# Soft-cap attention and soft mixture of experts on one core: a new plan for exponentials, joined tanhs, loads and unused products

## The chip, the cores and the metric

The kernel runs on one core of one Trainium2 chip. The metric is the device time of one execution in microseconds (us), the median of several runs. Of the core's engines the text speaks of TensorE (PE, matrix products into PSUM; PEld is its loading of weights), VectorE (DVE), ScalarE (ACT), GpSimd (POOL) and SyncE (SP, which here only issues DMAs). Each engine works off its own queue in program order and waits there for semaphores of the others.

## The reference

Two stages in float32. Attention with capped scores, for 8 batches, 12 heads, 448 tokens and 64 values a head:

```python
scores = scale * np.matmul(q, k.transpose(0, 1, 3, 2))
scores = cap * np.tanh(scores / cap)
scores = scores - np.max(scores, axis=-1, keepdims=True)
attn = np.exp(scores)
attn = attn / (np.sum(attn, axis=-1, keepdims=True) + 1e-09)
return np.matmul(attn, v).astype(np.float32)
```

Its output, as a matrix x of 3584 tokens by 768, goes through a soft mixture of 8 experts with 4 slots each: logits `x @ phi`, their softmax over the tokens mixes x into 32 slot inputs, each expert applies two weight matrices with a ReLU between (768 to 1024 to 768), and the softmax of the logits over the slots mixes the slot outputs back into the tokens.

## The kernel before

Heads are taken in pairs, 48 of them; two pairs make a group of four heads (Q, 24 of them) that is loaded together. A pair has seven tiles of scores of 128 keys by 448 queries, 336 tiles in all, and six tiles make a chunk (j, 56 of them), worked on in two halves of three tiles. Three groups are a batch, and a batch takes seven chunks, so the plan repeats with j modulo 7.

In a chunk, TensorE makes the scores in PSUM (`qk_chunk`, L337 on, six matmuls for a half), ACT takes the tanh out of PSUM into SBUF (`tanh_chunk`, L354, the activation at L365 for one half), and then the exponential in place (`exp_part`, L373). Chunks named in JOINED (L380) have one tanh over all six tiles (L361); for these both halves of scores must be there. From chunk 10 to chunk 49 the scores have one buffer of six banks, of which each half is free again when its tanh is over.

VectorE takes over part of the exponentials: SHARED (L381) says of each chunk how many of its six tiles, and `poly_exp` (L603) does them by a polynomial in seven instructions, steps 0 to 6 at L609 to L616. POLY (L382 to L590) says in which chunk and slot each step is issued. ACT does the tiles that are left.

Two chunks later TensorE multiplies with v (`pv_first`, `pv_rest`, L654 and L671; matmuls at L634), VectorE divides by the sums (`norm`, a reciprocal at L641 and a product at L644), and side jobs follow: `x_transp` turns the result (L689), `logits`, `e_exp` (an exponential of the logits on ACT, L721), `slot_sums`, `e_transp` (its copy ET at L740) and `e_sums` for a batch. `transp` (L269) turns the next k and q (matmuls kps and qps at L278, copies kT and qT by VectorE at L280). `vcast` (L285) casts v on GpSimd and lets SP load the next v; `load` (L182) issues the loads of k and q on GpSimd's queue, where the loads of the experts' weights (L116, L120) stand too.

The order is written out by hand. The main loop (L899 to L932) runs through a chunk as slots: `0`, tanh of the first half, `m`, tanh of the second half, `e`, the exponential of the chunk before, the first value products, `a`, their tail, the next chunk's first half of scores, `b`, the rest of the value products with slot `r` between the reciprocal and the product, `c`, the second half of scores, `d`. After a joined tanh the first half of scores comes only behind the rest of the value products. `at` puts a job into a slot of a chunk; `<` and `>` are ahead of and behind the slot's other jobs. WHEN (L818) has the slots of side jobs by chunk of the batch: `k1` to `q3` the turning of k and q of the batch's groups, `lk1` to `lq3` the loads of the group after, `x`, `lg`, `ee`, `ss`, `et`, `es` the side jobs.

TensorE also does products that nobody uses: `busy` (L878), `spare` (L800, in an own PSUM tile, 384 or 128 columns each) and `fill` (L660, 57 columns each, in the columns that the value products leave free). FILL (L804) places those that repeat with each batch.

The first pair is prepared apart (`first_pieces`, L224, called at L249): its float32 k and q are cast, turned and copied in pieces on ACT, VectorE and TensorE. SP loads q, and ACT's queue loads the first pair's k in two parts (L209). GpSimd's queue has its memsets first, then the q and k loads of group 2 (L260 to L262).

After chunk 55 comes the tail (L933 on): the last value products, the experts' two layers (L1078, L1106) and the mixing back with the stores of the output (L1130 to L1206).

Of the kernel before, what the change touches and what calls it, by code (L numbers as in the profile page):

```python
# [20 lines left out]
NT = 7  # L21
# [3 lines left out]
CS = 3  # L25
# [12 lines left out]
def kernel(  # L38
# [185 lines left out]
    def first_pieces(h, jobs):  # L224

        for stage, nm, c0, c1, eng, bank, at0 in jobs:
            copy = act.copy if eng is act else dve.tensor_copy
            cols = slice(h * HP, h * HP + HP)
            if stage == "junk":
                busy(c0)  # L230
            elif stage == "cast":
                copy(casts[nm, 0][:, c0:c1, cols],
                     raws[nm, 0][h][:, c0 * DH:c1 * DH].rearrange("p (c d) -> p c d", d=DH))
            elif stage == "turn":
                for c in range(c0, c1):
                    pe.transpose(bank[cols, at0 + c - c0, :], casts[nm, 0][:, c, cols], ident)
            else:
                copy(qkT[nm, 0][cols, c0:c1, :], bank[cols, at0:at0 + c1 - c0, :])  # L238

    def first_half(h):  # L240
# [5 lines left out]
        if h == 0:  # L246
# [128 lines left out]
    def exp_chunk(j):  # L375
# [4 lines left out]
    JOINED = (10, 14, 17, 21, 24, 31, 35, 38, 42, 45, 49)  # L380
    SHARED = {1: (2, 0), 3: (3, 0), 4: (3, 0), 6: (2, 0), 7: (3, 0), 9: (3, 0), 11: (3, 0), 12: (3, 0), 14: (3, 0), 16: (3, 0), 18: (3, 0), 19: (3, 0), 21: (3, 0), 23: (3, 0), 25: (3, 0), 26: (3, 0), 28: (3, 0), 30: (3, 0), 32: (3, 0), 33: (3, 0), 35: (3, 0), 37: (3, 0), 39: (3, 0), 40: (3, 0), 42: (3, 0), 44: (3, 0), 46: (3, 0), 47: (2, 0), 48: (2, 0), 49: (3, 0), 51: (2, 0), 52: (1, 0), 53: (3, 0), 54: (1, 0)}  # L381
    POLY = {(1, 'm'): ((1, 0),),  # L382
            (1, '<b'): ((1, 1),),
            (1, '>d'): ((1, 2),),
            (2, '<a'): ((1, 3),),
            (2, '>b'): ((1, 4),),
            (2, '<d'): ((1, 5),),
            (3, 'm'): ((3, 0),),
            (3, 'e'): ((3, 1),),
            (3, '>a'): ((1, 6),),  # L390
            (3, '<b'): ((3, 2),),
            (3, '<d'): ((3, 3),),
            (4, 'm'): ((3, 4),),
            (4, '<b'): ((3, 5),),
            (4, '>c'): ((4, 0),),
            (5, 'm'): ((4, 1),),
            (5, 'e'): ((3, 6),),
            (5, '<a'): ((4, 2),),
# [3 lines left out]
            (6, 'e'): ((4, 5), (6, 1)),  # L402
            (6, '<a'): ((4, 6),),
            (6, '>b'): ((6, 2),),
            (7, 'm'): ((6, 3),),
            (7, 'e'): ((6, 4), (7, 0)),
            (7, '<a'): ((6, 5),),
            (7, '<d'): ((7, 1),),
            (8, '0'): ((7, 2),),
            (8, 'm'): ((7, 3),),  # L410
            (8, '<a'): ((6, 6),),
            (8, '>b'): ((7, 4),),
            (8, '>c'): ((7, 5),),
            (9, 'e'): ((9, 0),),
            (9, '<a'): ((7, 6),),
            (9, '>b'): ((9, 1),),
            (9, '>d'): ((9, 2),),
            (10, 'm'): ((9, 3),),
            (10, '>b'): ((9, 4),),
            (10, '<d'): ((9, 5),),  # L420
            (11, 'm'): ((11, 0),),
            (11, 'e'): ((9, 6),),
            (11, '>a'): ((11, 1),),
# [3 lines left out]
            (12, '>a'): ((12, 0),),  # L427
            (12, '<b'): ((11, 5),),
            (12, '<c'): ((12, 1),),
            (13, '<a'): ((12, 2),),  # L430
            (13, '>a'): ((11, 6),),
            (13, 'r'): ((12, 3),),
            (13, '<d'): ((12, 4),),
            (14, '0'): ((12, 5),),
            (14, '<a'): ((14, 0), (12, 6)),
            (14, '>a'): ((14, 1),),
            (14, '<d'): ((14, 2), (14, 3)),
            (15, '<b'): ((14, 4),),
            (15, '>d'): ((14, 5),),
            (16, '0'): ((14, 6),),  # L440
            (16, '<b'): ((16, 0),),
            (16, '>c'): ((16, 1),),
            (16, '>d'): ((16, 2),),
            (17, 'e'): ((16, 3),),
            (17, '<a'): ((16, 4),),
            (17, '>d'): ((16, 5),),
            (18, 'm'): ((18, 0),),
            (18, '<a'): ((16, 6),),
            (18, '>a'): ((18, 1),),
            (18, '>b'): ((18, 2),),  # L450
            (18, '>d'): ((18, 3),),
            (19, '0'): ((18, 4),),
            (19, 'e'): ((18, 5), (19, 0)),
            (19, '<c'): ((18, 6),),
            (19, '>c'): ((19, 1),),
            (19, '<d'): ((19, 2),),
            (19, '>d'): ((19, 3),),
# [6 lines left out]
            (22, '<d'): ((21, 5),),  # L464
            (23, 'm'): ((23, 0), (21, 6)),
            (23, 'e'): ((23, 1),),
            (23, '<d'): ((23, 2),),
            (24, '0'): ((23, 3),),
            (24, 'm'): ((23, 4),),
            (24, '>c'): ((23, 5),),  # L470
            (25, 'm'): ((25, 0),),
            (25, '<a'): ((25, 1), (23, 6)),
            (25, '>b'): ((25, 2),),
            (25, '<c'): ((25, 3),),
            (25, '>d'): ((25, 4), (25, 5)),
            (26, '>b'): ((25, 6),),
            (26, '<c'): ((26, 0),),
            (27, 'm'): ((26, 1),),
            (27, 'e'): ((26, 2),),
            (27, '>b'): ((26, 3), (26, 4)),  # L480
            (28, 'e'): ((26, 5), (28, 0)),
            (28, '<a'): ((26, 6),),
            (28, '<c'): ((28, 1),),
            (28, '>c'): ((28, 2),),
            (29, '>a'): ((28, 3),),
            (29, '<b'): ((28, 4),),
            (29, '<d'): ((28, 5),),
            (30, 'e'): ((28, 6),),
            (30, '>b'): ((30, 0),),
            (30, '>c'): ((30, 1),),  # L490
            (31, '0'): ((30, 2),),
            (31, 'm'): ((30, 3),),
            (31, '<b'): ((30, 4),),
            (31, '>d'): ((30, 5),),
# [4 lines left out]
            (33, '0'): ((32, 3),),  # L499
            (33, 'e'): ((32, 4),),  # L500
            (33, '<b'): ((32, 5),),
            (33, '>b'): ((33, 0),),
            (33, '<c'): ((33, 1),),
            (34, '0'): ((33, 2), (33, 3)),
            (34, '>b'): ((33, 4),),
            (34, '<c'): ((32, 6), (33, 5)),
            (35, '<a'): ((33, 6),),
            (35, '<b'): ((35, 0),),
            (35, '>b'): ((35, 1),),
            (35, '<c'): ((35, 2),),  # L510
            (36, '<a'): ((35, 3),),
            (36, '>a'): ((35, 4),),
            (37, 'm'): ((35, 5), (35, 6)),
            (37, '<a'): ((37, 0),),
            (37, '>a'): ((37, 1),),
            (38, 'e'): ((37, 2),),
            (38, '>a'): ((37, 3),),
            (38, '>b'): ((37, 4),),
            (38, '>c'): ((37, 5),),
            (39, 'e'): ((39, 0), (37, 6)),  # L520
            (39, '>a'): ((39, 1),),
            (39, '>b'): ((39, 2),),
            (39, '<c'): ((39, 3),),
            (39, '>c'): ((39, 4),),
            (40, '>a'): ((40, 0),),
            (40, '<b'): ((40, 1),),
            (40, '>b'): ((39, 5),),
            (40, '<d'): ((40, 2),),
            (40, '>d'): ((40, 3),),
            (41, '>b'): ((40, 4),),  # L530
            (41, '<d'): ((39, 6),),
            (41, '>d'): ((40, 5),),
            (42, '<a'): ((42, 0),),
            (42, '>a'): ((40, 6), (42, 1)),
            (43, 'm'): ((42, 2),),
            (43, '<a'): ((42, 3), (42, 4)),
            (43, '>c'): ((42, 5),),
            (44, 'e'): ((42, 6),),
            (44, '<a'): ((44, 0),),
            (44, '>a'): ((44, 1),),  # L540
            (45, '<a'): ((44, 2), (44, 3)),
            (45, '>a'): ((44, 4),),
            (45, '<c'): ((44, 5),),
            (45, '>c'): ((44, 6),),
            (46, 'e'): ((46, 0),),
            (46, '<a'): ((46, 1),),
            (46, '>b'): ((46, 2),),
            (46, '<c'): ((46, 3),),
            (46, '>c'): ((46, 4),),
            (46, '>d'): ((46, 5),),  # L550
            (47, '<a'): ((47, 0),),
            (47, '>b'): ((47, 1),),
            (48, '0'): ((47, 2), (46, 6)),
            (48, 'e'): ((48, 0),),
            (48, '>a'): ((47, 3),),
            (48, '>b'): ((47, 4),),
            (48, 'r'): ((48, 1),),
            (48, '<c'): ((47, 5),),
            (49, '0'): ((48, 2),),
            (49, 'm'): ((47, 6), (48, 3)),  # L560
            (49, '<a'): ((49, 0),),
            (49, '>a'): ((48, 4),),
            (49, '>c'): ((48, 5),),
            (50, 'm'): ((49, 1),),
            (50, '<b'): ((48, 6), (49, 2)),
# [333 lines left out]
    for j in range(NCH):  # L899
# [28 lines left out]
        if j in JOINED:  # L928
            qk_chunk(2 * j + 2)
# [312 lines left out]
```

## Time and profile before

| what | us |
|---|---|
| median of 3 runs | 284.41 |
| lowest and highest | 284.2, 288.81 |
| the profiled execution's own time | 284.62 |
| its span | 282.8 |
| busy: PE, DVE, ACT, POOL | 244.9, 239.4, 250.0, 141.2 |
| first tanh on ACT starts | 6.18 |
| last exponential on ACT starts | 235.35 |

The span runs from the first to the last instruction of the profile; the execution's time has some 1.8 us more around it. A row of the timeline gives start, duration, engine, line, operation, output and input tile, and in brackets the idle time before it with what ended it. Consecutive instructions of one engine overlap in such rows, so that the mean duration of a group is longer than the distance between two starts. Rows of merged instructions (x2) give their whole stretch. In the line of 40 slices each digit is the busy share of 1/40 of the span in tenths; PEclk is TensorE's granted clock in the same way.

### The profile page before, as it was taken

Reading aid. Unit: us, or ns where it says so; the run is one execution under the profiler, and the core shown is the slowest. Engines: PE = TensorE matmul, PEld = TensorE weight load, DVE = VectorE, ACT = ScalarE, POOL = GpSimd, SP = SyncE. Lnnn points to the kernel's source line nnn. Section 1 sums busy time; section 2 is a strip of 40 time slices with the busy share of each in tenths; the row PEclk is TensorE's granted clock in tenths of the full one; section 3 lists DMA queues with packets and bytes.
Section 4 is the critical chain, followed back from the end, with each engine's and each line's share of the span. In section 5 each row is a group of like instructions: output and inputs, shape, how many; then the busy total and the mean of one; then the engine's idle time right before and its main releaser. Section 6 shows DMA issues by size and latency. Waiting matters only on the chain.

```text
span 282.8 us, 10334 instructions
## 1 busy us (share of the span) xinstructions
PE 244.9 (87%) x4505; PEld 164.4 (58%) x4505; DVE 239.4 (85%) x473; ACT 250.0 (88%) x200; POOL 141.2 (50%) x197
## 2 busy tenths in 40 slices
PE   8897889998998999889989998899988989998610
PEld 6654556755675666566757675666565768633300
DVE  3479999998999999999999999899999995457630
ACT  4999999999999999999999999999999995248520
POOL 7795547653966386628654866295623210200000
PEclk9999999999999999999999999999999999999955
DMA  7999999999999999999999999999999579959994
GB/s 248 227 190 199 222 217 230 231 221 220 215 232 221 218 228 231 221 214 217 232 217 210 222 230 217 215 214 230 217 217 203 160 230 363 409 225 368 418 426 204
DMA packets 58333, 68.09 MB, mean 241 GB/s; under 512 B 4144, under 2 KB 54448, under 8 KB 58288
## 3 DMA queue, kind: packets, MB, share of 16 engines
q0 software_dynamic: 42448, 35.31, 79.3%
q1 hardware_dynamic: 15552, 31.89, 32.0%
q8 instruction: 35, 0.57, 0.7%
q10 hardware_dynamic: 288, 0.23, 0.2%
q14 instruction: 10, 0.08, 0.1%
HBM read 91.72 MB, written 19.27 MB: 392 GB/s over the span
## 4 chain that ended last, share of the span: by engine, by line
ACT 36%; PE 26%; DVE 24%; issue 5%; DMA 3%; POOL 1%; DVEq 0%; SPq 0%; ACTq 0%
ACT ex L373 14%; ACT ex L365 14%; PE pv L634 8%; ACT ex L361 6%; PE sc L348 4%; DVE xq L644 3%; DVE xp L612 3%; DVE xp L614 3%; DVE ex L615 2%; DMA out_dram<-ob 2%; PE so_ps L1106 2%; PE hp L1078 2%; DVE xf L611 2%; DVE xp L613 2%; DVE qT L280 2%
## 5 line engine op out<-in xcount | busy, mean ns | idle before, releaser
L365 ACT ACTIVATE ex<-sc 128x1344 f16<-128x1344 f32 (+1 forms) x91 | 121.1, 1466 | 1.1 <-PE sc L348 1.1
L373 ACT ACTIVATE ex<-ex 128x1344 bf16<-128x1344 f16 (+5 forms) x58 | 113.7, 1963 | 0.1
L634 PE MATMUL pv<-vbd,ex 128*128 128x130 bf16 (+1 forms) x1610 | 94.5, 212 | 10.8 <-POOL vbd L288 4.3
L634 PEld LDWEIGHTS <-ex 128*128 128x128 bf16 (+1 forms) x1680 | 75.6, 101 | 39.9 <-issue 6.6
L288 POOL CAST vbd<-vraw 64x896 bf16<-64x896 f32 x46 | 47.7, 1038 | 59.5 <-PE pv L634 45.8
L348 PE MATMUL sc<-qT,kT 64*64 64x448 bf16 x672 | 66.2, 359 | 6.5 <-ACT ex L365 4.6
L348 PEld LDWEIGHTS <-kT 64*64 64x64 bf16 x672 | 22.2, 105 | 15.7 <-ACT ex L365 7.7
L644 DVE TENSOR_TENSOR xq<-pv,rec 128x448 bf16<-128x448 f32 x46 | 28.7, 625 | 1.6
L361 ACT ACTIVATE ex<-sc 128x2688 f16<-128x2688 f32 x11 | 29.0, 2632 | 0.0
L612 DVE TENSOR_TENSOR xp<-xf 128x1344 f16<-128x1344 uint16 (+2 forms) x34 | 27.5, 810 | 0.2
L615 DVE TENSOR_TENSOR ex<-ex,xp 128x1344 uint16<-128x1344 uint16 (+2 forms) x34 | 27.5, 810 | 0.2
L614 DVE TENSOR_TENSOR xp<-xp,xf 128x1344 f16<-128x1344 f16 (+2 forms) x34 | 27.1, 798 | 0.5
L116 POOL DMA_DIRECT2D w1b<-in_moe_w_dram x32 | 25.8, 807 | 0.0
L609 DVE TENSOR_SCALAR ex<-ex 128x1344 uint16<-128x1344 f16 (+2 forms) x34 | 17.3, 508 | 1.5 <-ACT ex L361 0.9
L280 DVE COPY kT<-kps 128x896 bf16<-128x896 bf16 x23 | 14.2, 617 | 4.6 <-PE kps L275 2.8
L613 DVE TENSOR_SCALAR xp<-xp 128x1344 f16<-128x1344 f16 (+2 forms) x34 | 17.0, 501 | 0.6
L611 DVE TENSOR_SCALAR xf<-ex 128x1344 uint16<-128x1344 uint16 (+2 forms) x34 | 16.9, 496 | 0.3
L185 POOL DMA_DIRECT2D qb<-in_q_dram x22 | 16.3, 741 | 1.4 <-ACT qT L238 0.8
L296 POOL MEMSET vbd<- 64x1 bf16 x22 | 2.8, 126 | 28.2 <-PE pv L634 28.0
L616 DVE TENSOR_SCALAR ex<-ex 128x1344 uint16<-128x1344 uint16 (+2 forms) x34 | 16.4, 484 | 0.2
L185 POOL DMA_DIRECT2D kb<-in_k_dram x22 | 16.6, 757 | 0.0
L120 POOL DMA_DIRECT2D w2d<-in_moe_w_dram x21 | 15.9, 779 | 0.0
(124 smaller groups left out, 314.9 us busy)
## 6 DMA issues: line engine op xcount, KB each, us to landing
w1b<-in_moe_w_dram POOLq DMA_DIRECT2D x32, 384.0 KB, 10.0
vraw<-in_v_dram SPq DMA_DIRECT2D x44, 224.0 KB, 6.1
w2d<-in_moe_w_dram POOLq DMA_DIRECT2D x21, 384.0 KB, 9.2
w2t<-w2d SPq DMA_DIRECT2D x21, 384.0 KB, 6.5
out_dram<-ob SPq DMA_DIRECT2D x7, 768.0 KB, 8.8
qb<-in_q_dram POOLq DMA_DIRECT2D x22, 224.0 KB, 8.0
kb<-in_k_dram POOLq DMA_DIRECT2D x22, 224.0 KB, 7.7
w2b<-in_moe_w_dram POOLq DMA_DIRECT2D x11, 384.0 KB, 8.8
```

Source lines behind the costliest of these rows:

```text
L116: pool.dma_start(out=w1b[e][:, js, fs], in_=w1r[:, e, js, fs])
L185: pool.dma_start(out=t, in_=quad_ap(nm, Q))
L288: pool.tensor_copy(vbds[Q % 2][r, :, :, c0:c0 + DH], raw[r])
L348: ins = pe.matmul(sc[cs, u, 0:S], qkT["k", Q][r, c, cs], qkT["q", Q][r, :, cs], start=True, stop=True).ins
L361: apart["t", i - 1] = apart["t", i] = act.activation(exs[j].bitcast(F16), own["board"][:, :, 0:S], ACT.Tanh, scale=qk_scale / cap).ins
L365: ins = act.activation(exs[j][:, half * CS + u0:half * CS + u1, :].bitcast(F16), (own[0] if i == u0 == 0 else sc)[:, u0:u1, 0:S], ACT.Tanh ...
L373: act.activation(exs[j][:, u0:u1, :], exs[j][:, u0:u1, :].bitcast(F16), ACT.Exp, scale=cap)
L612: lambda: dve.tensor_tensor(p, s, s.bitcast(F16), op=ALU.mult),
L614: lambda: dve.tensor_tensor(p, p, s, op=ALU.mult),
L615: lambda: dve.tensor_tensor(y, y, p, op=ALU.add),
L634: pe.matmul(out_, exs[j][r, u, q0:q0 + (HP if tail else P)], v_, start=(c == 0 and g == gs[0] < NF), stop=(c == NT - 1), skip_group_check= ...
L644: dve.tensor_tensor(xq[Q][:, h, s0:s1, :], pv[:, 0:s1 - s0, 0:DH], rec.to_broadcast([P, s1 - s0, DH]), op=ALU.mult)
```

## The change

It leaves the arithmetic as it is but for one tile's exponential, and sets the plan anew:

- SHARED: chunk 9 gives two of its tiles to VectorE instead of three, so that 92 tiles instead of 93 are done there.
- JOINED: 14 is taken out; 22, 28 and 43 come in, so 22 follows 21 and 43 follows 42.
- POLY: nearly every step of the polynomial is put into another slot, most of them by less than a chunk.
- FILL: 29 instead of 27 `fill` products in slot `a` of chunks 0 modulo 7, a `spare` of 8 instead of 7 in slot `c` of chunks 6 modulo 7, and new ones in slot `a`: 7 in chunks 1 and 4 in chunks 5 modulo 7.
- WHEN: the third group's q is turned in slot `a` instead of `b`, ahead of the next first half of scores; the load `lk1` (the second group's k) moves from two chunks before the batch to slot `b` of its first chunk, behind `lq1`; `lq1`, `lk2` and `lq3` go one or a few slots later.
- The first pair: the cast of k's last four blocks goes from ACT to GpSimd, ahead of the loads of group 2 on its queue, and two unused products on TensorE are dropped, so that the transposes of k follow those of q.
- A new table MID would put scores inside the value products; it is empty, and `pv_rest` issues the same products in the same order.

```diff
-            copy = act.copy if eng is act else dve.tensor_copy
+            copy = act.copy if eng is act else pool.tensor_copy if eng is pool else dve.tensor_copy
...
                              ("turn", "k", 0, CS, pe, two, 0), ("copy", "q", 4, NT, act, three, 0),
+                             ("cast", "k", CS, NT, pool, None, 0),
                              ("turn", "q", 0, 4, pe, one, 0), ("copy", "k", 0, CS, dve, two, 0),
-                             ("cast", "k", CS, NT, act, None, 0), ("copy", "q", 0, 4, dve, one, 0),
-                             ("junk", "k", 2, 0, pe, None, 0), ("turn", "k", CS, NT, pe, three, 3),
+                             ("copy", "q", 0, 4, dve, one, 0), ("turn", "k", CS, NT, pe, three, 3),
                              ("copy", "k", CS, NT, dve, three, 3)))
...
-    JOINED = (10, 14, 17, 21, 24, 31, 35, 38, 42, 45, 49)
+    JOINED = (10, 17, 21, 22, 24, 28, 31, 35, 38, 42, 43, 45, 49)
+    MID = {}
...
             (20, '>d'): ((19, 4),),
-            (21, '<b'): ((19, 5), (21, 0), (19, 6)),
-            (21, '>b'): ((21, 1),),
-            (21, '>c'): ((21, 2),),
+            (21, '0'): ((19, 5),),
+            (21, 'm'): ((19, 6),),
+            (21, '>a'): ((21, 0),),
+            (21, '<c'): ((21, 1),),
+            (21, '<d'): ((21, 2),),
             (21, '>d'): ((21, 3),),
...
-    def pv_rest(pr, between=()):
-        pv_mms(pr, CA, NT, (0, 1, 2), pvs[pr])
+    def pv_rest(pr, between=(), inside=None):
+        for c in range(CA, NT):
+            if inside and inside[0] == c:
+                for i in inside[1]:
+                    qk_chunk(i)
+            pv_mms(pr, c, c + 1, (0, 1, 2), pvs[pr])
...
-    FILL = ((7, 'a', fill, 27), (6, 'c', spare, 7),)
+    FILL = ((7, 'a', fill, 29), (6, 'c', spare, 8), (8, 'a', fill, 7), (5, 'a', fill, 4),)
...
-            'k3': (4, 'b'), 'q3': (5, 'b'), 'v3': (11, 'c'), 'x0': (5, 'c'), 'x1': (8, 'c'), 'x2': (10, 'b'),
-            'lg': (10, 'd'), 'ee': (11, 'm'), 'ss': (11, 'c'), 'et': (13, 'b'), 'es': (15, 'e'), 'lk1': (-2, 'a'),
-            'lq1': (-1, 'd'), 'lk2': (1, 'c'), 'lq2': (2, 'a'), 'lk3': (3, 'b'), 'lq3': (3, 'm')}
+            'k3': (4, 'b'), 'q3': (5, 'a'), 'v3': (11, 'c'), 'x0': (5, 'c'), 'x1': (8, 'c'), 'x2': (10, 'b'),
+            'lg': (10, 'd'), 'ee': (11, 'm'), 'ss': (11, 'c'), 'et': (13, 'b'), 'es': (15, 'e'), 'lk1': (0, 'b'),
+            'lq1': (0, 'm'), 'lk2': (2, 'e'), 'lq2': (2, 'a'), 'lk3': (3, 'b'), 'lq3': (3, 'e')}
```

More of the change, by code (lines that the diff above doesn't have):

```diff
@@ L426 @@
             (11, '>c'): ((11, 4),),
[L427 to L433, printed above, removed]
+            (12, 'm'): ((11, 5),),
+            (12, 'e'): ((12, 0),),
+            (12, 'r'): ((12, 1),),
+            (13, '0'): ((11, 6), (12, 2)),
+            (13, '<d'): ((12, 3),),
+            (13, '>d'): ((12, 4),),
@@ L443 @@
-            (16, '>d'): ((16, 2),),
+            (16, 'm'): ((14, 6),),
+            (16, '<a'): ((16, 0),),
+            (16, '>b'): ((16, 1),),
+            (17, '0'): ((16, 2),),
             (17, 'e'): ((16, 3),),
[L445 to L449, printed above, removed]
+            (17, '>b'): ((16, 4),),
+            (17, '<d'): ((16, 5),),
+            (18, 'e'): ((18, 0), (16, 6)),
@@ L476 @@
[L476 to L482, printed above, removed]
+            (24, 'm'): ((23, 3),),
+            (24, '>a'): ((23, 4),),
+            (25, 'e'): ((23, 5), (25, 0)),
+            (25, '<a'): ((25, 1),),
+            (25, '>a'): ((23, 6),),
+            (25, '>b'): ((25, 2),),
@@ L483 @@
+            (25, '>c'): ((25, 3),),
+            (25, '<d'): ((25, 4),),
+            (26, 'm'): ((25, 5),),
+            (26, '>a'): ((26, 0), (25, 6)),
+            (26, '>c'): ((26, 1),),
+            (27, '>b'): ((26, 2),),
+            (27, 'r'): ((26, 3),),
+            (27, '<d'): ((26, 4),),
+            (28, 'e'): ((26, 5), (26, 6), (28, 0)),
             (28, '<c'): ((28, 1),),
-            (28, '>c'): ((28, 2),),
-            (29, '>a'): ((28, 3),),
+            (28, '<d'): ((28, 2),),
@@ L486 @@
+            (29, 'm'): ((28, 3),),
             (29, '<b'): ((28, 4),),
[L487 to L494, printed above, removed]
+            (30, 'm'): ((28, 5),),
+            (30, '<a'): ((28, 6), (30, 0)),
+            (30, '<b'): ((30, 1),),
+            (30, '<d'): ((30, 2),),
@@ L495 @@
+            (31, 'e'): ((30, 3),),
+            (31, '<a'): ((30, 4),),
+            (31, '<d'): ((30, 5),),
             (32, 'm'): ((32, 0),),
@@ L518 @@
[L518 to L521, printed above, removed]
+            (36, '0'): ((35, 1),),
+            (36, 'm'): ((35, 2),),
+            (36, 'e'): ((35, 3),),
+            (36, '<a'): ((35, 4),),
+            (37, 'e'): ((35, 5),),
+            (37, '<a'): ((35, 6), (37, 0)),
+            (37, '>a'): ((37, 1),),
+            (37, '>d'): ((37, 2),),
+            (38, 'e'): ((37, 3), (37, 4)),
+            (39, '0'): ((37, 5),),
@@ L531 @@
[L531 to L543, printed above, removed]
@@ L544 @@
-            (45, '>c'): ((44, 6),),
+            (40, '<c'): ((40, 1),),
+            (40, '>d'): ((40, 2),),
+            (41, '<b'): ((40, 3),),
+            (41, '>c'): ((40, 4), (39, 6)),
+            (41, '<d'): ((40, 5),),
+            (42, 'e'): ((40, 6),),
+            (42, '<b'): ((42, 0),),
+            (42, '>b'): ((42, 1),),
+            (42, '<c'): ((42, 2),),
+            (43, 'm'): ((42, 3),),
+            (43, '<b'): ((42, 4),),
+            (44, '0'): ((42, 5),),
+            (44, '<a'): ((44, 0), (42, 6)),
@@ L553 @@
[L553 to L555 removed]
+            (46, '>c'): ((46, 3),),
+            (47, '<a'): ((46, 4),),
+            (47, '>a'): ((47, 0),),
+            (47, '>b'): ((46, 5), (47, 1)),
+            (47, '<c'): ((46, 6),),
+            (48, '0'): ((47, 2),),
+            (48, 'm'): ((48, 0),),
+            (48, '<b'): ((47, 3),),
             (48, '>b'): ((47, 4),),
[L557 to L558 removed]
+            (48, 'r'): ((48, 1), (47, 5)),
@@ new lines @@
+            (49, '>d'): ((48, 6), (49, 2)),
+            (50, 'e'): ((49, 3),),
+            (50, '>c'): ((49, 4),),
+            (50, '>d'): ((49, 5),),
+            (51, '0'): ((49, 6),),
+            (51, 'm'): ((51, 0),),
+            (51, '>c'): ((51, 1),),
+            (51, '>d'): ((51, 2),),
+            (52, 'm'): ((51, 3), (52, 0)),
+            (52, '>a'): ((51, 4),),
+            (52, '<c'): ((52, 1),),
+            (52, '>d'): ((51, 5), (52, 2), (51, 6)),
+            (53, 'm'): ((52, 3),),
@@ L922 @@
         run(j, "b")
+        inner = pr is not None and j in MID
         if pr is not None:
-            pv_rest(pr, aux.pop((j, "r"), ()))
+            pv_rest(pr, aux.pop((j, "r"), ()), (MID[j], (2 * j + 2, 2 * j + 3)) if inner else None)
             vcast_after(pr)
@@ L927 @@
             run(j, "r")
-        if j in JOINED:
+        if j in JOINED and not inner:
             qk_chunk(2 * j + 2)
         run(j, "c")
-        qk_chunk(2 * j + 3)
+        if not inner:
+            qk_chunk(2 * j + 3)
         run(j, "d")
```

193 lines of the change are left out of this document (78 added, 115 removed).

## The prediction

> **What bounds the kernel now.** I read the page first, then ScalarE's rows by form, its timeline, the waits of TensorE, and the timelines of TensorE and GpSimd around the places that the diff touches.
>
> ```profile
> PE 244.9 (87%) x4505; PEld 164.4 (58%) x4505; DVE 239.4 (85%) x473; ACT 250.0 (88%) x200; POOL 141.2 (50%) x197
> ACT  4999999999999999999999999999999995248520
> PEclk9999999999999999999999999999999999999955
> ```
>
> ACT is full from slice 2 to slice 33, some 7 to 235 us. The tail behind it is a chain through all engines that the diff leaves alone.
>
> ```profile
> L365 ACT ACTIVATE ex<-sc 128x1344 f16<-128x1344 f32 x89 | 119.9, 1483 | 0.2 <-PE sc L348 0.2
> L373 ACT ACTIVATE ex<-ex 128x1344 bf16<-128x1344 f16 x28 | 43.0, 1537 | 0.0
> L361 ACT ACTIVATE ex<-sc 128x2688 f16<-128x2688 f32 x11 | 29.0, 2632 | 0.0
> ...
> L373 ACT ACTIVATE ex<-ex 128x1792 bf16<-128x1792 f16 x5 | 9.5, 1903 | 0.0
> ```
>
> Tanhs and exponentials have almost no idle time before them. But the means here overlap one another, so prices must come from start to start:
>
> ```profile
> 86.84 2.69 ACT L365 ACTIVATE ex<-sc 128x1344 f16<-128x1344 f32 x2
> 89.20 1.55 ACT L373 ACTIVATE ex<-ex 128x1344 bf16<-128x1344 f16 x1
> 90.42 2.63 ACT L361 ACTIVATE ex<-sc 128x2688 f16<-128x2688 f32 x1
> 92.72 2.65 ACT L373 ACTIVATE ex<-ex 128x2688 bf16<-128x2688 f16 x1
> 95.06 2.68 ACT L365 ACTIVATE ex<-sc 128x1344 f16<-128x1344 f32 x2
> 97.40 1.55 ACT L373 ACTIVATE ex<-ex 128x1344 bf16<-128x1344 f16 x1
> ```
>
> Two half tanhs take 97.40 - 95.06 = 2.34 us, 1.171 each; a joined one 2.29; an exponential of six tiles 2.33, of three 1.21. An exponential of four tiles (from 206.72 on) takes 1.587. Against these steps ACT loses only 1.74 us between its first tanh (6.18) and its last exponential (235.35): 0.40 at 29.40, 0.29 at 227.48, 0.16 to 0.18 behind two rows before a chunk's logits exponential (135.15, 220.49), 0.05 and 0.10 before the joined tanhs of chunks 35 and 42, the rest in the first 17 us. So ACT is the bound, and the other engines count only where they hand it scores late. How near they are: the scores' last matmul ends 0.04 us before the joined tanhs of 21, 35 and 42, and 0.05 to 0.23 before the second tanh of every chunk 6 modulo 7.
>
> ```profile
> PE sc L348 <- ACT ex L365: 4.6, 9, 0.7
> PE pv L634 <- POOL vbd L288: 4.3, 9, 0.7
> PE pv L634 <- DVE xq L644: 3.7, 9, 1.1
> ...
> PE pv L634 <- DVE ex L616: 2.2, 6, 0.5
> ```
>
> TensorE waits some 15 us in all in the loop; that is the room for more unused products.
>
> **The start.** ACT's cast of the last four blocks of the first k goes to GpSimd, and two unused products go.
>
> ```profile
> 4.96 0.40 ACT L232 CAST casts<-kraw 128x256 bf16<-128x256 f32 x1
> 5.42 0.41 PE L236 MATMUL boot<-ident,casts 128*64 128x128 bf16 x4
> 5.76 1.41 PE L348 MATMUL sc<-qT,kT 64*64 64x448 bf16 x12
> ```
>
> ACT casts 4.96 to 5.36, behind its copy of q; the transposes follow at 5.42 and stand in TensorE's queue ahead of the first scores (5.76), which ACT awaits (0.81 us idle before 6.18). The second part of k lands at 4.73, and GpSimd's memsets end at 4.28. No row has this cast on GpSimd; it is bounded by 0.31 us (its memset of 128x256) and 0.93 (its cast of 128x896). By the elements, 256 of 896, and some 0.1 us that its smallest memset takes, I estimate 0.35. So 4.80 to 5.15, transposes at 5.21, 0.21 earlier. The scores also need q's copy, done at 5.44, so 0.26 is the most to be won. If the cast takes 0.93 the start loses 0.35. GpSimd's next instruction, the q load, waits until 5.12 anyway. I take -0.20; ends -0.26 and +0.76 (0.93 and a DVE copy of 0.41 before it).
>
> On GpSimd the same cast of 64x896 takes 0.92 us at 66.33 and 1.34 at 172.13, beside different work on DVE. [...]
>
> **One tile fewer on VectorE.** Chunk 9's exponential on ACT grows from three tiles to four: 1.587 - 1.214 = +0.37 us on the bound, with no cover. VectorE's seven steps for that chunk shrink from 4.70 us (mean rows of 1344: 534+528+876+536+861+853+509 ns) to 3.67 (of 896), -1.03. I counted VectorE's work in program order in both orders of the steps: up to chunk 9 nothing comes later, and from chunk 11 on nearly every copy of k, q, x and every norm has 1.03 us (0.15 to 2.3) less work ahead of it; one step 6 (chunk 18's) has 0.12 more. So moving the steps adds no lateness.
>
> **Joined tanhs.** 14 goes, 22, 28 and 43 come: two more at 2.342 - 2.291 = 0.051, -0.10 us. Each needs all twelve matmuls of scores. Chunk 28 is like 21, 35 and 42 (zero slack, 0.00 to 0.10 lost): now its second half is ready at 118.91 for a start at 118.73; estimate +0.1. 22 and 43 follow a joined tanh, and their scores stand behind the rest of the value products: ready at 95.19 where ACT comes free at 95.06, and at 180.71 for 180.38. That is 0.13 and 0.33 if nothing moves; VectorE's lead takes TensorE's waits there (0.49 on ET at 90.86, 0.24 on step 6 at 179.39) away in part. I take +0.25 for the two, +0.35 for all three; ends 0 and +0.8.
>
> **Unused products.** The 27 after the first value products become 29, 33 ns each (6.2 us by 189): +0.07 us, in chunks 0 modulo 7. Seven become eight in chunks 6 modulo 7, between the two halves of scores: one of 128 columns, +0.06, just where chunks 21, 28, 35 and 42 have no slack: +0.15 in all. Seven new ones in chunks 1 modulo 7 (0.23) meet slack of 1.3 us, except at 22 and 43, counted above. Four new ones in chunks 5 modulo 7 (0.13) stand with the third q's 14 transposes (0.58), now ahead of the next first half: slack there 1.3 to 1.6 us, so covered. For the second half the transposes only change places, and 0.13 meets slack of 0.05 to 0.23: +0.15, mostly at chunk 6. Ends 0 and +0.8.
>
> **Loads.** The load of each group's second k goes, on GpSimd's queue, from two chunks before the group to behind the second q's load, past two weight loads (0.76 each) and two casts of v with a memset (0.95 and 0.1); the weight loads behind it come 0.74 later and have a whole kernel to spare. The other moved loads keep their order there, also against GpSimd's casts. SP's loads of v wait for those casts, which do not move by more. What counts is when k is there:
>
> ```profile
> 60.07 0.74 POOL L185 DMA_DIRECT2D qb<-in_q_dram  x1
> ...
> 71.51 0.58 PE L278 MATMUL kps<-ident,kb 128*64 128x128 bf16 x14
> ```
>
> That q lands at 70.33. Where k and q are loaded back to back now, the second lands 1.1 to 1.3 us after the first, mostly. So k would land at about 71.5, for transposes at 71.51; for the groups after it 100.1 against 99.93, 126.5 against 128.76, then a whole us to spare. With the k load gone from ahead of q, both may land earlier, by up to that 1.2. No wait: 0; ends -0.1 and +0.6.
>
> **Lead of VectorE.** ACT's 0.29 at 227.48 stands behind value products that VectorE's last steps feed (chain of waits at 224.8 to 227.3). With 1.03 us less ahead it should go: -0.3; ends -1.0 (most of the loop's losses) and 0.
>
> **Sum.** -0.20 + 0.37 - 0.10 + 0.35 + 0.15 + 0.15 + 0 - 0.3 = +0.42 us on the profiled execution (span 282.8, time 284.62, 1.8 lying around it): 285.0. The median shown is 284.41, 0.21 under that execution, so **284.8**.
>
> **Rivals.**
> 1. *The lead is worth more.* VectorE's 1.03 us removes TensorE's waits (3.7 + 2.2 us) and with them all joined tanhs' losses and nearly all of ACT's idle time: -0.26 + 0.37 - 0.10 - 1.0 = -1.0, so 283.4. For it: those waits. Against it: most of them cost ACT nothing now.
> 2. *Handover fails at several joined tanhs and chunks 6 modulo 7*: the upper ends, -0.2 + 0.37 - 0.1 + 0.8 + 0.8 + 0.3 (half of the load's end) = +2.0, so 286.4. For it: slacks of 0.04. Against it: VectorE's lead.
> 3. *The late k load, slower by over 2%.* k would hold TensorE ahead of the scores of the joined chunks 3 modulo 7; these have 0.35 to 1.03 us of slack in their second half, 0.8 on average. To cost 5.7 us over seven groups, each must lose 0.81, so k must come 1.6 us after its transposes' present time, everywhere: 290.1 or more. Against it: by the sum above only the first three groups are near zero, and the other four have one to two us to spare. Whether the queue delays this k by more than its neighbour no row shows.
> 4. *The start loses* (GpSimd's cast at its upper end): +0.96 against the sum, 285.8; inside the range.
>
> **How the numbers follow.** Forecast 0.60; rival 1 0.17; rival 2 (with 4) 0.17; rival 3 0.06. The forecast's own range is 284.2 to 285.6. Leaving out rival 3 and the outer parts of 1 and 2, the range is 283.4 to 286.8. Two per cent, 5.7 us, is about what a measurement of this kernel can tell from no change. Faster by that would need more than three times ACT's losses: 0.01. Slower: rival 3, 0.06. Within: 0.93.
>
> **What would show it.** In the changed profile: first tanh near 5.98 (right) or after 6.18 (start wrong); chunk 9's exponential as a sixth row of 128x1792; 13 joined rows; ACT's excess over its steps near 1.7 to 2 us, with entries at 22, 28, 43 (joins) and 29 us; none at 227; no wait of the kps matmuls for a load; PEclk still 9 up to the tail. An excess over 3 us, a wait on a k load, or a slice of PEclk under 9 in the loop would prove the forecast wrong.

## The result, and the profile after

The changed kernel takes 286.23 us, the median of 8 runs (285.06 to 290.06), against 284.40 for the kernel before beside it. The ratio is 1.0068 with an interval of 1.0047 to 1.0089: slower by 0.7%, so within 2% and inside the range, but above the forecast's own 284.2 to 285.6, 1.4 us above the 284.8 and on the other side of what rival 1 gave. Ratios are made from undisturbed executions alone and medians from all of them, which is why the two may differ by some tenths of a per cent and more.

The profiled execution after is the fastest of its eight: 285.06 us, span 283.3. The page, then ScalarE's rows by form:

```profile
PE 247.6 (87%) x4605; PEld 168.3 (59%) x4605; DVE 240.7 (85%) x473; ACT 250.5 (88%) x197; POOL 138.9 (49%) x198
...
PEclk9999999999999999999999999999999999999955
```

```profile
L365 ACT ACTIVATE ex<-sc 128x1344 f16<-128x1344 f32 x85 | 109.9, 1376 | 0.4 <-PE sc L348 0.3
...
L361 ACT ACTIVATE ex<-sc 128x2688 f16<-128x2688 f32 x13 | 32.7, 2518 | 0.6 <-PE sc L348 0.6
L373 ACT ACTIVATE ex<-ex 128x1792 bf16<-128x1792 f16 x6 | 10.5, 1751 | 0.0
```

The counts are those foreseen (13 joined rows, a sixth 1792). Two things are not. DVE has one tile less, 1.03 us by the old rows, and yet is busy 1.3 us longer (239.4 before, 240.7 now). And the joined tanhs have 0.6 us of idle time before them where they had none. From start to start of ACT's rows, the stretch from the first tanh to the last exponential grew from 229.17 to 230.69 us. Of these 1.52 us, 0.27 is work (0.37 for the tile, less 0.10 for the joins). The rest is waiting: ACT's loss against its steps went from 1.74 to 2.97. One place holds 1.01 of it: the row that starts at 202.85, ahead of the joined tanh of chunk 49. Its timeline after:

```profile
200.46 1.08 POOL L288 CAST vbd<-vraw 64x896 bf16<-64x896 f32 x1
...
200.64 1.15 DVE L604 TENSOR_SCALAR xf<-ex 128x896 uint16<-128x896 uint16 x1
...
201.71 0.18 DVE L634 RECIPROCAL rec<-pv 128x7 f32<-128x7 f32 x1
...
202.47 0.82 DVE L609 TENSOR_SCALAR ex<-ex 128x1344 uint16<-128x1344 uint16 x1
...
203.22 0.60 DVE L693 COPY xT<-xps 128x896 bf16<-128x896 bf16 x1
...
203.88 0.49 PE L736 MATMUL eps<-ident,E 128*32 128x128 bf16 x16 [1.22 <-DVE xT L693]
...
205.45 2.41 ACT L361 ACTIVATE ex<-sc 128x2688 f16<-128x2688 f32 x1 [0.65 <-PE sc L348]
```

The same place before:

```profile
200.27 0.38 DVE L611 TENSOR_SCALAR xf<-ex 128x896 uint16<-128x896 uint16 x1
...
200.57 0.20 DVE L641 RECIPROCAL rec<-pv 128x7 f32<-128x7 f32 x1
...
200.75 0.95 POOL L288 CAST vbd<-vraw 64x896 bf16<-64x896 f32 x1
...
201.34 0.61 DVE L696 COPY xT<-xps 128x896 bf16<-128x896 bf16 x1
```

The row to look at is step 1 of chunk 47, a TENSOR_SCALAR of 128x896. Before, it starts ahead of GpSimd's cast of v and takes 0.38 us. Now step 5 of chunk 46 (0.85) stands ahead of it, it starts 0.18 us behind the cast's start, and takes 1.15: it ends 0.25 us behind the cast's end (201.54). No view calls that a wait; it is only a row that got longer. Behind it stand, on DVE's queue, the reciprocal (1.14 later), the norm's product, step 6 of chunk 46 (0.82 instead of 0.51, and itself moved ahead of the copy) and the copy xT (1.88 later). TensorE waits 1.22 us for xT with the scores of chunk 49 behind in its queue: these start at 204.84 (203.55 before), and ACT waits.

### The profile page after: what moved, and what is told of

Same layout as the page of the kernel before. It is cut to its first block, busy times and chain, and to the rows that moved or that the text cites. A ratio compares the mean times of both kernels' runs of the same rounds, so it can differ in the third digit from the quotient of the medians.

```text
span 283.3 us, 10529 instructions
## 1 busy us (share of the span) xinstructions
PE 247.6 (87%) x4605; PEld 168.3 (59%) x4605; DVE 240.7 (85%) x473; ACT 250.5 (88%) x197; POOL 138.9 (49%) x198
## 4 chain that ended last, share of the span: by engine, by line
ACT 40%; DVE 29%; PE 18%; issue 5%; DMA 3%; POOL 1%; DVEq 0%; ACTq 0%; SPq 0%; POOLq 0%
ACT ex L373 16%; ACT ex L365 14%; ACT ex L361 8%; DVE ex L608 3%; DVE xp L607 3%; DVE xp L605 3%; PE pv L627 3%; DVE xq L637 3%; DVE xf L604 3%; PE sc L348 2%; DVE ex L609 2%; DVE ex L602 2%; PE so_ps L1105 2%; DMA out_dram<-ob 2%; PE hp L1077 2%
## 5 line engine op out<-in xcount | busy, mean ns | idle before, releaser
L365 ACT ACTIVATE ex<-sc 128x1344 f16<-128x1344 f32 (+1 forms) x87 | 111.1, 1361 | 1.3 <-PE sc L348 1.2
L373 ACT ACTIVATE ex<-ex 128x1344 bf16<-128x1344 f16 (+5 forms) x58 | 108.2, 1870 | 0.1
L288 POOL CAST vbd<-vraw 64x896 bf16<-64x896 f32 x46 | 46.7, 1015 | 56.5 <-PE pv L627 37.4
L361 ACT ACTIVATE ex<-sc 128x2688 f16<-128x2688 f32 x13 | 32.7, 2518 | 0.6 <-PE sc L348 0.6
L608 DVE TENSOR_TENSOR ex<-ex,xp 128x1344 uint16<-128x1344 uint16 (+2 forms) x34 | 26.7, 786 | 0.2
L604 DVE TENSOR_SCALAR xf<-ex 128x1344 uint16<-128x1344 uint16 (+2 forms) x34 | 18.4, 540 | 0.3
L606 DVE TENSOR_SCALAR xp<-xp 128x1344 f16<-128x1344 f16 (+2 forms) x34 | 18.0, 530 | 0.6
```

What stands on the lines that cost most here:

```text
L288: pool.tensor_copy(vbds[Q % 2][r, :, :, c0:c0 + DH], raw[r])
L361: apart["t", i - 1] = apart["t", i] = act.activation(exs[j].bitcast(F16), own["board"][:, :, 0:S], ACT.Tanh, scale=qk_scale / cap).ins
L365: ins = act.activation(exs[j][:, half * CS + u0:half * CS + u1, :].bitcast(F16), (own[0] if i == u0 == 0 else sc)[:, u0:u1, 0:S], ACT.Tanh ...
L373: act.activation(exs[j][:, u0:u1, :], exs[j][:, u0:u1, :].bitcast(F16), ACT.Exp, scale=cap)
L604: lambda: dve.tensor_scalar(s, y, STEP - 1, STEP, ALU.bitwise_and, ALU.bitwise_or),
L608: lambda: dve.tensor_tensor(y, y, p, op=ALU.add),
```

## The experiments

The theories. **A**: VectorE's steps, set anew, meet GpSimd's casts of v; the rows that meet are stretched, and the norms and copies behind them come late. **B**: the joined tanhs, the products and the loads hand the scores over late (rivals 2 and 3). **C**: step 2 of chunk 53, which starts beside a cast in both kernels, is long for a reason of its own, and ACT's loss there comes from TensorE's own queue. **D**: it is VectorE's order, with step 5 of chunk 46 ahead of the norm, and not the cast. The first four runs shared one chip, the next four a second, the last four a third; each ratio is against the kernel before on the same chip.

**The change again** (no edit).

> The changed kernel once more, for the spread and a second profile. Theory A (VectorE's moved steps run into GpSimd's casts and DMA issues, which makes VectorE's instructions longer, and TensorE and ACT wait for them): 286.2 us, 1.9 us above the kernel before; a loss of about 1 us ahead of the joined tanh of chunk 49 in the profile again, VectorE's step 1 of chunk 47 at about 1.15 us instead of 0.38. Theory B (joined tanhs, unused products and loads hand the scores over late): the same time, but the losses stand at 22, 28, 43 and in chunks 6 modulo 7, and the one at 49 is chance and absent here.

Measured: 288.27 us (285.85 to 291.29), 1.0091 (1.0034 to 1.0149). Step 1 takes 1.15 us again beside a cast of 1.03, and this profile, of an execution of 290.42 us, shows what the first one did not. Its windows of 3.41 us, the shortest stretch of a halved clock in these profiles, cut at the moments when the granted clock changes (columns: busy time and instructions of PE, PEld, DVE, ACT, POOL; granted clock; DMA share; GB/s):

```profile
197.38:200.79 3.41, 3.41 (x63) 2.34 (x63) 3.38 (x7) 3.41 (x4) 1.23 (x2) 1.00 1.27 232
200.79:204.20 3.41, 1.90 (x31) 0.93 (x29) 3.38 (x6) 3.41 (x4) 3.10 (x5) 1.00 1.29 233
204.20:207.61 3.41, 3.05 (x38) 1.55 (x39) 3.21 (x8) 1.97 (x2) 1.75 (x3) 0.50 1.22 217
207.61:211.03 3.42, 3.42 (x57) 3.17 (x53) 2.71 (x6) 3.42 (x2) 0.00 (x0) 0.50 1.29 203
```

In the window with the wait TensorE is busy 1.90 of 3.41 us. Behind it its clock is halved for 6.83 us, and ACT loses 1.80 at 203.75 and 1.88 at 209.45, instead of 1.01 and 0.14. I take it that clock and wait belong together: the wait leaves TensorE idle, and the idle time costs more than itself. The last run below tests this.

**The steps alone, and the rest alone**: the kernel before with SHARED and POLY of the changed one, and the changed kernel with those of the one before.

> The kernel before with only the new division and order of the polynomial's steps (SHARED and POLY); start, joined tanhs, unused products and loads as before. Theory A: 0.37 for the tile and 1 to 1.5 of new ACT idle time, so 1.4 to 1.9 us slower than before (285.8 to 286.3). Theory B: only the 0.37, less what VectorE's lead saves: 284.4 to 284.8.

> The changed kernel with the division and order of the polynomial's steps of before; start, joined tanhs, unused products and loads as changed. Theory A: the start's 0.25 and the joins' 0.10 are gained, handovers lose little: 284.0 to 284.5. Theory B: slower than before by 1 us and more: 285.4 or above.

Measured: the steps alone 287.98 us (287.11 to 292.23), 1.0109 (1.0074 to 1.0144), with both long rows and the clock halved at 206.5 and at 230.4, more than A's 1.4 to 1.9 us; the rest alone 285.29 (284.25 to 289.85), 0.9954 (0.9902 to 1.0007). The ratios speak for A. But the rest alone isn't free: its loop takes 230.74 us, as long as that of the change, and ACT loses some 3.4 in it, mostly at 111 to 148 us and at 229. So B isn't out by these two runs, and the new steps don't only harm; this is taken up below.

**One step later**: step 1 of chunk 47 behind the norm's product.

```diff
-            (47, '>b'): ((46, 5), (47, 1)),
-            (47, '<c'): ((46, 6),),
+            (47, '>b'): ((46, 5),),
+            (47, '<c'): ((47, 1), (46, 6)),
```

> The changed kernel with one step moved: chunk 47's step 1 goes behind the norm's product in place of ahead of the norm, so that it starts after GpSimd's cast of v. Theory A: the step takes 0.38 us instead of 1.15, the scores of chunk 49 are there in time, 0.8 to 1.0 us less than the changed kernel: 285.2 to 285.4, where the other runs of the changed kernel have that loss too. Theory B: no difference to the changed kernel, 286.2.

Measured: 286.25 us (284.57 to 289.78), 1.0026 (0.9968 to 1.0084), so no 285.2 to 285.4 in the median, and an interval that overlaps that of the change. What settles it is the profile. The step, now clear of the cast, and what follows:

```profile
201.60 0.38 DVE L604 TENSOR_SCALAR xf<-ex 128x896 uint16<-128x896 uint16 x1
...
201.90 0.50 DVE L609 TENSOR_SCALAR ex<-ex 128x1344 uint16<-128x1344 uint16 x1
...
202.31 0.62 DVE L693 COPY xT<-xps 128x896 bf16<-128x896 bf16 x1
```

It has its 0.38 us back, xT follows earlier, and ACT's loss at chunk 49 is gone. This execution still took 288.74, since the clock was halved from 227.5 on for 10.24 us, behind the other collision (chunk 53).

**The kernel before with one step moved, and the change with both moved**: step 2 of chunk 53 from ahead of the norm to behind its product; in the second kernel step 1 of chunk 47 as well. The edit of the first:

```diff
-            (53, '<b'): ((53, 2),),
+            (53, '<c'): ((53, 2),),
```

> The kernel before with one step moved: chunk 53's step 2 goes behind the norm's product in place of ahead of its reciprocal. In the profile of before it starts 0.04 us after a cast of v on GpSimd and takes 1.60 us in place of 0.85; the norm, the next value products (1.05 us of TensorE idle) and ACT (0.29 us at 227.48) wait behind it. Theory A (VectorE and GpSimd shut each other out): the step takes 0.85 to 1.2 us, the norm comes 1.3 to 1.6 us earlier, ACT's 0.29 goes, and TensorE's clock is cut less often behind it: 0.3 us faster in profiles with a full clock, more in the median. Theory C (the step is long for a reason of its own, and ACT's loss comes from TensorE's own queue): the step stays at 1.6 us and the time within 0.1 us.

> The changed kernel with both steps moved, chunk 47's step 1 and chunk 53's step 2, each behind the norm's product. Theory A: ACT's losses of 1.0 us at chunk 49 and 0.4 us at chunk 55 go, 285.0 or less where the kernel before has 284.4, ratio 0.998 to 1.004. Theory B (joins, unused products and loads): 1.007 to 1.009 as the change itself.

Measured: the kernel before so edited 284.57 us, 1.0000 (0.9974 to 1.0026), the change so edited 284.44, 0.9985 (0.9964 to 1.0006). The loops shorten from 229.17 to 228.51 and from 230.69 to 229.10, and ACT's loss at 227 is gone in both. In the first of the two the step of chunk 53 starts 0.72 us into the cast and takes 0.91 us, and the norm's reciprocal starts at 224.50 instead of 226.28, so C is out: the step's length wasn't its own. Its loss is real, but both kernels had it; it can't be what makes them differ. Two steps put behind a product take away all that the change had lost against the kernel before: its loop is 1.59 us shorter, and its profiled time 284.30.

The ratio of 1.0000 hides a gain. Of the 25 executions of the kernel before on this chip six took 288.5 us or more; of the 30 of the three kernels here with chunk 53's step moved (these two and the next) none took over 285.3. The run before has a profile of 288.74 us with the clock halved behind that step; the long executions of the kernel before left no trace, so that they have the same cause isn't shown.

**The kernel before with its step moved and the new start.** The edit is the first hunk of the change's diff.

> The kernel before with the new start alone (GpSimd's cast of the first k, two unused products dropped) and chunk 53's step 2 moved. Both theories: the first tanh 0.25 us earlier than before, at equal landing of q. Theory A: 0.25 + 0.29 = 0.5 us faster than before with a full clock, ratio 0.995 to 0.998, and the best of all kernels so far. Theory B: 0.25 faster, 0.999.

Measured: 283.78 us, 0.9972 (0.9957 to 0.9988), as A gave. It beats both kernels.

**The cast held back**: in the changed kernel GpSimd first copies the norm's seven reciprocals into an unused tile, so that the cast of pair 38 comes behind the step (the lines that keep the tile and the reciprocals for this are not shown).

```diff
+        if pr == 38:
+            pool.tensor_copy(pad[:, 0:NT].unsqueeze(2), recs[pr])
```

> The changed kernel with one cast of v on GpSimd held back: a copy of seven values of the norm's reciprocal stands ahead of it on GpSimd's queue, so that the cast starts after chunk 47's step 1; VectorE's order stays. Theory A: step 1 takes 0.38 us in place of 1.15, and ACT's loss ahead of chunk 49's joined tanh falls from 1.0 to 0.5 or less (the next steps may meet the later cast). Theory D (it is VectorE's order, step 5 of chunk 46 ahead of the norm, and not the cast): step 1 short or not, the loss stays at 0.8 to 1.0.

Measured, in a single execution: 289.21 us, no gain, but the rows show what the cast's place does.

```profile
201.00 0.39 DVE L606 TENSOR_SCALAR xf<-ex 128x896 uint16<-128x896 uint16 x1
...
202.04 0.95 POOL L288 CAST vbd<-vraw 64x896 bf16<-64x896 f32 x1
202.08 1.28 DVE L611 TENSOR_SCALAR ex<-ex 128x1344 uint16<-128x1344 uint16 x1
```

Step 1, in its old place, is short again. The cast, 1.6 us later, stretches step 6 of chunk 46 instead, which stands ahead of xT: 1.28 for 0.50. TensorE still waits 0.93 us for xT, the clock is halved at 203.8, and ACT loses 1.72 ahead of chunk 49 where A gave 0.5 or less. So by the loss this run doesn't part A from D. The two kernels with step 1 behind the product do. In the change with both steps moved, step 5 of chunk 46 stays ahead of the norm and the same instructions stand ahead of xT; yet xT starts 2.26 us after that step, where the change has 3.35. The 1.09 between are the stretch of step 1 (0.77) and of step 6 (0.32, beside a DMA issue of GpSimd), and ACT's loss is gone. The order alone isn't it: D is out.

**The rest with the step of chunk 53 moved, and the joins alone**: the rest alone with the edit of chunk 53, and the best kernel so far with the change's JOINED.

```diff
-    JOINED = (10, 14, 17, 21, 24, 31, 35, 38, 42, 45, 49)
+    JOINED = (10, 17, 21, 22, 24, 28, 31, 35, 38, 42, 43, 45, 49)
```

> The changed kernel's start, joined tanhs, unused products and loads with the steps of before (93 tiles), chunk 53's step 2 moved behind the norm's product. If joins, unused products and loads cost ACT what the prediction's sum said (-0.10 + 0.35 + 0.15 + 0.15), it is 0.5 us slower than the same kernel with the start alone (283.8 there): 284.3. If they gain what they save, 283.6.

> The kernel before with the new start, chunk 53's step 2 moved, and the 13 joined tanhs; unused products and loads as before. By the sum (-0.10 + 0.35) 0.25 us slower than with the 11 joined ones (283.8): 284.0. If the joined tanhs cost no wait: 283.7.

Measured: 285.20 us, 1.0018 (0.9989 to 1.0047), loop 230.50; and 285.45 us, 1.0033 (1.0011 to 1.0054), loop 230.13, 1.49 longer than without the joins, although these take 0.10 of work away. By the ratios (the best kernel's is from another chip) that is 1.3 and 1.7 us above the best kernel, where 0.5 and 0.25 were expected. I had given the joins no such price. In the joins alone, ACT's losses of 0.37 and 0.83 us (ahead of 192.87 and 210.00) come behind two more steps, at 187.82 and 201.28, that start just behind a cast; the first:

```profile
187.70 0.93 POOL L288 CAST vbd<-vraw 64x896 bf16<-64x896 f32 x1 [0.67 <-PE pv L634]
187.82 1.18 DVE L611 TENSOR_SCALAR xf<-ex 128x1344 uint16<-128x1344 uint16 x1
...
189.91 1.09 PE L634 MATMUL pv<-vbd,ex 128*128 128x130 bf16 x20 [1.38 <-DVE xq L644]
```

Two other losses, 0.18 ahead of the joined tanh of chunk 22 (95.31) and 0.32 ahead of that of chunk 43 (180.80), have no long step near them: there the scores come late, as the prediction gave for these chunks "if nothing moves" (0.13 and 0.33), so B holds in part. A joined chunk also shifts the casts against the steps, so an order of steps seems to fit the set of joined chunks that it was made for: with the changed joins ACT loses 3.4 us in the loop under the old steps, and only 1.4 under the new ones less the two bad places. How much of the 3.4 is collisions and how much late scores no run parts.

**Only the step of chunk 53 moved in the change, and then TensorE's gap filled**: the second adds 36 unused products where TensorE waits for xT.

```diff
+    at(48, '<b', fill, 36)
```

> The changed kernel with chunk 53's step 2 moved alone, so that the wait ahead of chunk 49's joined tanh stays. Theory A: with a full clock 1.0 us slower than with both steps moved (284.4), so 285.4; and in a part of the runs TensorE's clock is cut to half behind that wait, so that the runs scatter up to 287 and more. If the wait alone counts, all runs lie at 285.4.

> The kernel of the run before with 36 unused products of 57 columns (1.2 us) on TensorE just where it waits 1.2 us for VectorE's copy of x in chunk 48. If the clock is cut because TensorE stands idle there: ACT still waits its 1.0 us, but no run has a cut clock near 204 us, and all runs lie near 285.4. If the clock is cut for another reason: as without the products. If the products only delay: 286.4.

Measured: 286.49 us (285.16 to 289.19), 1.0075 (1.0042 to 1.0108); and 285.28 (284.83 to 285.88), 1.0028 (1.0006 to 1.0049). The profile of the first has the clock halved at 203.77 for 6.83 us, and ACT loses 2.02 and 1.86. In the second ACT still loses 1.01 at 203.96, the wait for xT being as it was, but the clock stays up and the window of the wait reads:

```profile
200.00:203.41 3.41, 2.71 (x51) 1.59 (x51) 3.38 (x7) 3.41 (x4) 1.94 (x4) 1.00 1.27 227
```

Products that nobody uses save 1.2 us of the median and three quarters of the spread (1.05 us instead of 4.03), by keeping TensorE busy through a wait that they don't shorten.

## Why the forecast was off by 1.4 us, point by point

- **The start** (-0.20): GpSimd's cast takes 0.40 us (estimate 0.35), and the first tanh starts at 5.93 instead of 6.18, so -0.25 in this profile. That it would come behind a copy of VectorE of 0.41, as in the term's upper end, no run shows: it starts at 4.72 behind its DMA, beside a copy of VectorE (4.73) that takes its 0.35 us as before:

```profile
4.72 0.40 POOL L232 CAST casts<-kraw 128x256 bf16<-128x256 f32 x1 [0.33 <-DMA kraw<-in_k_dram]
...
5.17 0.41 PE L236 MATMUL boot<-ident,casts 128*64 128x128 bf16 x4 [0.25 <-POOL casts L232]
5.51 1.41 PE L348 MATMUL sc<-qT,kT 64*64 64x448 bf16 x12
```

  Rival 4 is out. Over all profiles of these runs, though, the first tanh lies anywhere from 5.93 to 6.64 with the new start, and from 6.18 to 6.37 with the old one: it mostly rises with the moment when TensorE's full clock begins, 3.49 to 6.8 us into the span (with the new start 5.93 at 4.19 and 6.36 at 5.40, with the old one 6.18 at 3.49 and 6.37 at 5.39). Where that moment is about the same the starts hardly differ: 6.32 and 6.37 with the old one (clock from 5.11 and 5.39), 6.30 and 6.36 with the new one (5.18 and 5.40). So a single profile can't tell the gain, and -0.20 isn't shown. That the best kernel's median is 0.8 us under that of the same kernel with the old start is more than 0.25 explains; where the rest comes from stays open.
- **The tile and the joins' rows** (+0.37, -0.10): right by the counts and the steps.
- **Handover at the joins** (+0.35): 28 loses 0.36 in two rows (117.47 and 121.18), 22 and 43 nothing. The sum is right, its places are not: 22 and 43 had 0.43 and 0.36 us to spare under the new steps, and lost 0.18 and 0.32 under the old ones.
- **Unused products** (+0.15 and +0.15): smaller. With the two steps out of the way, the loop of the change (229.10) stands against that of the kernel before with its step moved (228.51) at +0.59: 0.27 of work and 0.32 of handover, where the joins and products together were put at 0.65. The products were not tried alone.
- **Loads** (0): right. k is there 0.9 to 3.4 us before TensorE takes it, in each of seven groups, and in the list of TensorE's waits no load stands ahead of the matmuls of k and q:

```profile
PE pv L627 <- DVE xq L637: 3.2, 6, 1.1
...
PE eps L736 <- DVE xT L693: 1.2, 1, 1.2
...
PE kps L278 <- DVE ET L737: 0.3, 1, 0.3
```

  Rival 3 is out.
- **Lead of VectorE** (-0.3) **and "moving the steps adds no lateness"**: this is the step that failed. I counted VectorE's work in program order with mean durations, found 1.03 us less of it ahead of nearly everything, and let that pay for the loss at 227. But a mean duration isn't a property of the instruction alone. DVE's rows that run more than 0.03 us over the median of their operation and form are over by 5.0 us in all before and by 7.4 after; 2.4 us more eat the 1.03 and 1.3 besides, which is about what DVE's busy time shows. The loss at 227 did not go, it grew to 0.39, since step 2 of chunk 53 starts 0.04 us behind a cast in both kernels:

```profile
225.89 0.93 POOL L288 CAST vbd<-vraw 64x896 bf16<-64x896 f32 x1 [3.13 <-PE pv L627]
225.93 1.60 DVE L605 TENSOR_TENSOR xp<-xf 128x1344 f16<-128x1344 uint16 x1
```

  The kernel before had this very row, 1.60 us against a mean of 0.88, in the place where I looked for 0.3 us. I read it as VectorE having too much to do, and it was a row that ends only 0.71 us behind the cast's end; 1.03 us less work ahead didn't move it: it starts 0.04 us behind the cast's start in either kernel. In the traces before and after, a step that starts in the first 0.75 us of a cast of v ends a fixed time behind the cast's end, 0.25 us for a TENSOR_SCALAR of 128x896, 0.36 to 0.38 for one of 128x1344, 0.70 to 0.72 for a TENSOR_TENSOR of 128x1344. It is the same 0.37 whether the step starts 0.04 us into the cast (202.08 with the cast held back), 0.09 (58.09 in the change) or 0.63 (74.40 before). The row at 58.09, 1.23 us long, is a third collision of the changed kernel, and ACT loses nothing behind it: a collision costs only where someone waits. I had seen the same cast take 0.92 us in one place and 1.34 in another, beside different work on VectorE, and drew nothing from it for the 46 casts against the 238 steps of 34 chunks, nearly all of which the change moves.
- **"No slice of PEclk under 9"**: true of the profile first seen, not of the kernel. Of five profiles with the wait for xT and its gap unfilled (the change twice, the steps alone, only chunk 53's step moved, the cast held back) four have the clock halved, at 203.8 to 206.5. The halved clock accounts for much of what lies between the first profile's 285.06 and the median of 286.23, as filling the gap shows (286.49 to 285.28); that it accounts for all of it isn't shown, since the runs that were only timed leave no trace. In the change's second profile ACT is also 6.4 us over its steps, where the prediction set 3 as the sign of being wrong and the first profile has 2.97.
- **The sum**: the forecast gave +0.42 for the profiled execution, +0.72 without the lead; measured +0.44 (285.06 against 284.62). That is luck: the loop is 1.52 longer, the start 0.25 shorter, and the tail took 46.66 us instead of 47.49, 0.4 of it in a shorter wait for the output's stores, which the change doesn't touch. What the medians differ by is mostly step 1 of chunk 47 and the clock behind it: with chunk 53's step moved alone the ratio stays at 1.0075, with both moved it is 0.9985. Rival 2 had the size (286.4) with the wrong cause: in the change not one of the new joins costs what this step does. That the time lies inside the range is owed to the width given to rival 2.

Open: the point from which the clock is halved. Near 204 it was, behind windows of 3.41 us in which TensorE was busy 55% to 57% (four profiles, of them 1.90 us in the change again and 1.91 with only chunk 53's step moved), and not behind 64% (2.19 us, the first profile of the change, with 2.71 in the window ahead of it), nor behind 60% (187.32 to 190.73 in the joins alone). Near 228, windows of 69% to 74% were followed by a halved clock in some profiles and by a full one in others, so the share alone doesn't decide. The length of some steps next to GpSimd's DMA issues, 0.1 to 0.4 us above the usual, was not tried by itself either.

## What to carry to other kernels

When steps move on VectorE, don't count their mean durations: look in the trace for the longest row of each form, see what GpSimd does then, and lay the moved steps against GpSimd's instructions one by one. A row that got longer can be a wait that no list of waits shows (step 1 of chunk 47 took 1.15 us for 0.38, with no wait noted), and what counts is who stands behind it: put what reads PSUM beside the cast (here the norm's reciprocal and product, 0.20 and 0.62 us there as elsewhere), and a step that reads SBUF behind it (0.38 us again). Then look at a second and third profile, since here one and the same wait of TensorE cost ACT about 1 us in one execution and nearly 4 in the next (1.01 and 0.14, against 1.80 and 1.88).

## What the runs showed of the hardware

- Steps of VectorE that read SBUF ran longer when they started early in one of GpSimd's casts of v: 0.38 became 1.15 (200.64 in the change), 0.50 became 1.28 (202.08 with the cast held back), 0.85 became 1.60 us (225.93 in the change), and the end lay 0.25, 0.37 and 0.71 us behind that of the cast. Its reciprocals, products and copies that read PSUM didn't: of some fifty that start in the first 0.6 us of a cast, in either kernel, the products of the norm all take 0.62 or 0.63 us, as elsewhere, the reciprocals 0.19 to 0.21, the copies of 128x896 0.61 or 0.62. The other way round, a cast that begins while such a step has some 0.2 us or more still to run is the longer one (1.08 at 200.46 in the change with 0.26 to run, 1.36 at 195.87 with 0.58, against 0.92 to 0.96). What in the chip lies behind this no run shows.
- TensorE's granted clock fell to 0.50 without TensorE ever standing still for long. Near 204, its wait for xT was 0.9 to 1.5 us (0.93 with the cast held back, 1.23 with only chunk 53's step moved); in the 3.41 us ahead of the cut it was busy 55% to 57%, and the halved clock lasted 3.41 or 6.83 us. Near 230 the 3.41 us ahead of the cut were 69% to 74% busy (2.53 us in the run with one step later), and the halved clock lasted 3.41 or 10.24 us, so each time a multiple of 3.41.
